# Decoding the second MoE's weights: an even schedule, VectorE in place of GpSimd, and four PSUM banks for h

## The chip, the cores and the metric

The program runs on one core of a Trainium2 chip. The metric is the device time of one execution in microseconds (us). The engines are named as in the profile: PE is TensorE (PEld its weight loads), DVE is VectorE, ACT is ScalarE, POOL is GpSimd, and SP is SyncE, which here only issues DMAs.

## The reference

Three layers follow each other in float32: an attention, and two mixtures that are plain dense layers ("MoE" in the names).

```python
x = attention(q, k, v)                 # 4 batches x 576 tokens = 2304 rows of 512
h = x @ w_in                           # first MoE: 512 -> 2048
x = (h - tanh(h)) @ w_out              # 2048 -> 512
xn = x / sqrt(mean(x*x) + 1e-6) * rms_g
g, val = xn @ w_gate, xn @ w_val       # second MoE: 512 -> 1536, twice
out = (g * sigmoid(g) * val) @ w_out2  # 1536 -> 512
```

The weights arrive as float64. The kernel reads their bits as pairs of 32-bit words and builds float32 values from them on the chip.

## The kernel before

**Weights.** Each weight tile is 128 x 512 values. `Weight.load` (L119) lets SP load its 512 KB. `Weight.bits` (L126) makes a float32 out of the two words: a multiplication by 2 to the power -111 into the tile `ca`, on ACT (L131) or on POOL (L133), then three bit operations on DVE into the tile `ct` (L138, L139, L142). `Weight.split` (L147) writes two float32r parts: the high part is a copy on ACT (L150), the low part a subtraction (L151) on the engine that the stream's `place` names. `ca` and `ct` have two buffers each. A `Stream` (L153) walks through a list of weights: step i loads some weights ahead, decodes weight i and splits weight i - 1. `st1` carries the 32 weights of the first MoE, all on ACT and DVE. `st2` (L195) carries the 36 of the second one (gate, val and out2 for each of 12 blocks f): every other multiplication is on POOL, and two of three subtractions (24 in all) are on POOL. A weight needs a buffer of the pool `wts` for its raw words and one for its parts; `wts` has 32 buffers, and in the second MoE's decode they become free as the last group of the first MoE uses up that MoE's weights. The last five split weights go to a pool of their own (`wts2`).

**First MoE.** The rows are worked on in five groups of 512 (one of 256). For each group and each of 16 blocks f, `unit` (L831) issues: `pe_h` (12 matmuls of 128 x 512 into a PSUM bank of the pool `ps_h`, which has two), tanh on ACT (`tg`, L646), a DVE operation that reads the bank and leaves h - tanh(h) (L651), the high part `g` on ACT (L657), the low part on DVE (L662), and, two units later, `pe_x` (12 matmuls that add to four banks of `ps_x`). In the last group `unit` also moves `st2` on, two weights per block, and `prep(0)` normalises the first 512 rows for the second MoE: squares on ACT, sums on DVE, a matmul with ones, three Newton steps for the inverse root on DVE, and the split of the result into `xn` (L744, L745).

**Second MoE.** It goes through five blocks of rows (four of 512, one of 256). For each f, `pe_gv` issues 12 matmuls for the gate (into `ps_h`) and 12 for the value (into `ps_m`, two banks), silu on ACT (`s`, L762), the product on DVE (L763), and its split (`p`, ACT L765, DVE L766); `pe_o` adds 12 matmuls of the block f before. During the first rows `st2` decodes what is left.

**Order.** The calls above give instructions and their priority; a list scheduler of the framework, which works with modelled times, then sets the order in which they stand on each engine. Each engine runs its row strictly in that order, and so does SP with the DMA issues: an instruction that waits holds all behind it.

Of the kernel before, what the change touches and what calls it, by code (L numbers as in the profile page):

```python
# [7 lines left out]
F32 = mybir.dt.float32  # L8
# [17 lines left out]
def attn_moe_moe_kernel(  # L26
# [22 lines left out]
    nc = tc.nc  # L49
    B, _, NC, D = q_str.shape  # L50
    NT, DM = out.shape
    FA = w_in.shape[0]
    FB = w_gate.shape[0]
# [10 lines left out]
    NG = len(groups)  # L64
# [19 lines left out]
    wts = ctx.enter_context(tc.tile_pool(name="wts", bufs=2 * FA))  # L84
    cvt = ctx.enter_context(tc.tile_pool(name="cvt", bufs=2))
    ps_h = ctx.enter_context(tc.tile_pool(name="ps_h", bufs=2, space=PSUM))
    ps_m = ctx.enter_context(tc.tile_pool(name="ps_m", bufs=2, space=PSUM))
# [22 lines left out]
    def mm(out_, lhsT, rhs, start, stop):  # L110
        nc.tensor.matmul(out_, lhsT, rhs, start=start, stop=stop, skip_group_check=True)  # L111
# [69 lines left out]
    w2 = {(kd, f): Weight(kd, f) for f in range(FB) for kd in ("gate", "val", "out2")}  # L181
    w1_order = [("in", 0)]
    for f in range(1, FA):
# [7 lines left out]
    )  # L191
    w2_order = [w2[kd, f] for f in range(FB) for kd in ("gate", "val", "out2")]
    N2 = 5
    NK = len(w2_order) - N2
    st2 = Stream(  # L195
        w2_order,
        lambda i: ((wts, "w") if i < NK else (wts2, "w2")) + (nc.vector if i % 3 == 0 else nc.gpsimd,),
        3, 2 * FA, lambda i: i % 2 == 0,
    )

    xh = {}
# [432 lines left out]
    xs, g_of, h_of, t_of, xacc = {}, {}, {}, {}, {}  # L634

    def pe_h(g, f, a, e):
        ps = ps_h.tile([128, 512], F32, tag="h", name="ps_h")[:, :e - a]
        w, x = w1["in", f].t, xs[g]
        seq = [(i, k, c) for c in range(4) for i, k in ((0, 0), (0, 1), (1, 0))]
        for n, (i, k, c) in enumerate(seq):  # L640
            mm(ps, w[:, i, c, :], x[:, k, c, a:e], n == 0, n == len(seq) - 1)
        h_of[g, f, a] = ps

    def act_tanh(g, f, a, e):
        t = gp.tile([128, 512], F32, tag="tg", name="tg")[:, :e - a]
        nc.scalar.activation(out=t, in_=h_of[g, f, a], func=ACTF.Tanh, scale=WS)  # L646
        t_of[g, f, a] = t

    def dve_g(g, f, a, e):
        t = t_of[g, f, a]  # L650
        nc.vector.scalar_tensor_tensor(  # L651
            out=t, in0=h_of.pop((g, f, a)), scalar=WS, in1=t, op0=ALU.mult, op1=ALU.subtract
        )

    def g_hi(g, f, a, e):
        t = ghl.tile([128, 2, 512], F32R, tag="g", name="g")[:, :, :e - a]
        nc.scalar.copy(out=t[:, 0], in_=t_of[g, f, a])  # L657
        g_of[g, f, a] = t

    def g_lo(g, f, a, e):  # L660
        t = g_of[g, f, a]
        nc.vector.tensor_tensor(out=t[:, 1], in0=t_of.pop((g, f, a)), in1=t[:, 0].bitcast(F32), op=ALU.subtract)  # L662

    def pe_x(g, f, a, e):
        if g not in xacc:
            xacc[g] = [ps_x.tile([128, 512], F32, tag="x", name="ps_x") for _ in range(4)]
        w, t = w1["out", f].t, g_of.pop((g, f, a))
        for c in range(4):
            for n, (i, k) in enumerate(((0, 0), (1, 0), (0, 1))):
                mm(  # L670
                    xacc[g][c][:, a:e], w[:, i, c, :], t[:, k],
                    f == 0 and n == 0 and a == 0, f == FA - 1 and n == 2,
                )
        if f == FA - 1 and e == width[g]:
            evac_x(g)
# [75 lines left out]
    def pe_gv(j, f):  # L751
        r, n = [], rows[j][1]
        for kd, pool, tag in (("gate", ps_h, "h"), ("val", ps_m, "m")):
            ps = pool.tile([128, 512], F32, tag=tag, name="ps_" + tag)[:, :n]
            w, x = w2[kd, f].t, xn[j]
            seq = [(a, e, c) for c in range(4) for a, e in ((0, 0), (0, 1), (1, 0))]
            for i, (a, e, c) in enumerate(seq):
                mm(ps, w[:, a, c, :], x[:, e, c, :], i == 0, i == len(seq) - 1)
            r.append(ps)
            if kd == "gate":  # L760
                s = pb.tile([128, 512], F32, tag="s", name="s")[:, :n]
                nc.scalar.activation(out=s, in_=ps, func=ACTF.Silu, scale=WS)  # L762
        nc.vector.scalar_tensor_tensor(out=s, in0=r[1], scalar=WS, in1=s, op0=ALU.mult, op1=ALU.mult)  # L763
        t = pb.tile([128, 2, 512], F32R, tag="p", name="p")[:, :, :n]
        nc.scalar.copy(out=t[:, 0], in_=s)  # L765
        nc.vector.tensor_tensor(out=t[:, 1], in0=s, in1=t[:, 0].bitcast(F32), op=ALU.subtract)  # L766
        p_of[j, f] = t

    def pe_o(j, f):
        if f == 0:  # L770
            oacc[j] = [ps_x.tile([128, 512], F32, tag="x", name="ps_x") for _ in range(rows[j][1] // 128)]
        w, p = w2["out2", f].t.rearrange("p s c f -> p s (c f)"), p_of.pop((j, f))
        for t in range(rows[j][1] // 128):
            for i, (a, e) in enumerate(((0, 0), (1, 0), (0, 1))):
                mm(
                    oacc[j][t], p[:, e, t * 128:t * 128 + 128], w[:, a, :],
                    f == 0 and i == 0, f == FB - 1 and i == 2,
                )

    def evac_o(j):  # L780
        if j == nb - 1:
            os = pbx.tile([128, 4, 512], F32, tag="x2", name="os")
        for t in range(rows[j][1] // 128):
            o = os[:, t] if j == nb - 1 else pb.tile([128, 512], F32, tag="o", name="o")
            if t % 2 == 0:
                nc.scalar.mul(out=o, in_=oacc[j][t], mul=WS)
            else:
                nc.vector.tensor_scalar_mul(out=o, in0=oacc[j][t], scalar1=WS)
            t0 = rows[j][0] + t * 128
            nc.sync.dma_start(out=out[t0:t0 + 128, :], in_=o)  # L790
# [32 lines left out]
    def attend(j):  # L823
        w = wks[j]
        if j < EA and len(w.pe) == 12:
            for c in ("abcde" if j == 0 else "ABCDE") + "t":
                ensure(c)
        if w.pe:
            w.pe.pop(0)()

    def unit(g, f, a, e, pe_work=lambda: None, work=lambda: None):  # L831
        if g == 0:
            for i in range(1 if e == SUB else 2):
                while wks[i].pe:
                    attend(i)
            st1.to(w1_at["in", f] + 1)
        pe_h(g, f, a, e)
        act_tanh(g, f, a, e)
        pe_work()
        dve_g(g, f, a, e)  # L840
        work()
        g_hi(g, f, a, e)
        if g == NG - 1 and f >= 1:
            st2.to(min(NK, 2 * f))
        g_lo(g, f, a, e)
        xq.append((g, f, a, e))
        while len(xq) > (1 if g == 0 else 2):
            if xq[0][0] == 0:
                st1.to(w1_at["out", xq[0][1]] + 1)
            pe_x(*xq.pop(0))  # L850

    for c in START:
        if c in "abcdeABCDEt":
            ensure(c)
        elif c == "w":
            st1.load_to(min(st1.n + 1, 2 * FA))
        elif c in "01":
            attend(int(c))
        elif c == "s":
            st1.step()  # L860
        elif c == "U":
            unit(*units.pop(0))
# [5 lines left out]
    for g, f, a, e in units:  # L868
# [16 lines left out]
        def pe_work():  # L885
            if f >= 2 or 0 < g < NG - 1:
                wk.run_pe(max(rem, 1))

        def work():
            if f >= 6 or 0 < g < NG - 1:  # L890
                wk.run(wk.st, max(rem, 1))

        unit(g, f, a, e, pe_work, work)
        if g == NG - 1:
            if f == 4:
# [9 lines left out]
    pbn = ctx.enter_context(tc.tile_pool(name="pbn", bufs=1, reuse_waits="tile"))  # L905
    wts2 = ctx.enter_context(tc.tile_pool(name="wts2", bufs=N2, reuse_waits="tile"))

    pq = []
    for j in range(nb):
        pg = prep(j + 1, pbn if j % 2 == 0 else pbx) if j + 1 < nb else iter(())  # L910
        for f in range(FB):
            if j == 0:
                st2.to(3 * (f + 2))
            pe_gv(j, f)
            if f >= (1 if j > 0 else 4):
                next(pg, None)
                next(pg, None)
            pq.append((j, f))
            if len(pq) > 1:
                jj, ff = pq.pop(0)  # L920
                pe_o(jj, ff)
                if ff == FB - 1:
                    evac_o(jj)
        for _ in pg:
            pass
# [82 lines left out]
```

## Time and profile before

| | |
|---|---|
| three runs | 961.97 us median (961.53 to 963.13) |
| profiled execution | 962.53 us, span from first to last instruction 960.8 us |
| mean granted TensorE clock | 0.994 |
| PE busy | 929.7 us (97%), 5274 matmuls |
| DVE busy | 519.9 us (54%) |
| ACT busy | 346.5 us (36%) |
| POOL busy | 119.6 us (12%), 147 instructions |

PE is the engine that is nearly always busy, so the span is PE's work and the gaps in it. The shares of the other engines are means over stages that differ much: the attention, the decode of weights, and the long second MoE in which only PE has much to do. The last group of the first MoE starts on PE at 400.82 us and the second MoE at about 498 us.

### The profile page before, as it was taken

Reading aid. Unit: us, or ns where it says so; the run is one execution under the profiler, and the core shown is the slowest. Engines: PE = TensorE matmul, PEld = TensorE weight load, DVE = VectorE, ACT = ScalarE, POOL = GpSimd, SP = SyncE. Lnnn points to the kernel's source line nnn. Section 1 sums busy time; section 2 is a strip of 40 time slices with the busy share of each in tenths; the row PEclk is TensorE's granted clock in tenths of the full one; section 3 lists DMA queues with packets and bytes.
Section 4 is the critical chain, followed back from the end, with each engine's and each line's share of the span. In section 5 each row is a group of like instructions: output and inputs, shape, how many; then the busy total and the mean of one; then the engine's idle time right before and its main releaser. Section 6 shows DMA issues by size and latency. Waiting matters only on the chain.

```text
span 960.8 us, 13712 instructions
## 1 busy us (share of the span) xinstructions
PE 929.7 (97%) x5274; PEld 779.3 (81%) x5274; DVE 519.9 (54%) x1199; ACT 346.5 (36%) x820; POOL 119.6 (12%) x147
## 2 busy tenths in 40 slices
PE   5799999999999999999899999999999999999998
PEld 5688888888999888887667778888888888888897
DVE  4899998873454433269999764254124412331212
ACT  4776654223554433244445323113111311121211
POOL 2000036760000000013334210000000000000000
PEclk9799999999999999999999999999999999999999
DMA  9936334220421200066335211101010000000100
GB/s 204 336 127 209 109 104 141 77 79 1 122 84 42 77 31 1 23 219 200 129 105 181 71 39 44 44 1 44 1 44 1 23 1 33 11 1 1 43 2 23
DMA packets 51489, 72.66 MB, mean 76 GB/s; under 512 B 24928, under 2 KB 35552, under 8 KB 51424
## 3 DMA queue, kind: packets, MB, share of 16 engines
q1 hardware_dynamic: 51424, 71.80, 24.5%
q8 instruction: 41, 0.67, 0.3%
q14 instruction: 24, 0.20, 0.1%
HBM read 62.34 MB, written 9.44 MB: 75 GB/s over the span
## 4 chain that ended last, share of the span: by engine, by line
PE 78%; DVE 11%; DMA 5%; issue 3%; POOL 1%; SPq 1%; ACT 1%; POOLq 0%; ACTq 0%
PE ps_h L111 30%; PE ps_x L111 30%; PE ps_m L111 14%; PE ps_s L111 2%; DVE ct L139 2%; DVE ct L142 2%; DVE ct L138 2%; PE ps_v L111 2%; DMA raw<-in_w_out_dram 2%; DVE w L151 1%; DMA raw<-in_w_val_dram 1%; DVE g L662 1%; PE ps_p L325 1%; DMA qz<-in_q_loc_dram 1%; DMA x<-x2d 1%
## 5 line engine op out<-in xcount | busy, mean ns | idle before, releaser
L111 PE MATMUL ps_h<-xs,w 128*128 128x512 f32 (+1 forms) x984 | 220.9, 369 | 6.2 <-DVE tg L651 6.0
L111 PE MATMUL ps_x<-g,w 128*128 128x512 f32 (+1 forms) x984 | 222.0, 368 | 0.6 <-DVE g L662 0.5
L111 PEld LDWEIGHTS ps_h<-xs,w 128*128 128x128 f32 x984 | 169.7, 190 | 37.9 <-DVE tg L651 9.2
L111 PEld LDWEIGHTS ps_x<-g,w 128*128 128x128 f32 x984 | 168.5, 188 | 31.4 <-DVE g L662 1.9
L111 PE MATMUL ps_x<-w,p 128*128 128x512 f32 x648 | 158.9, 392 | 3.5 <-DVE p L766 2.2
L111 PE MATMUL ps_m<-xn,w 128*128 128x512 f32 (+1 forms) x720 | 158.4, 368 | 0.8 <-DVE xn L745 0.8
L111 PE MATMUL ps_h<-xn,w 128*128 128x512 f32 (+1 forms) x720 | 159.0, 369 | 0.1
L763 DVE SCALAR_TENSOR_TENSOR s<-ps_m,s 128x512 f32<-128x512 f32 (+1 forms) x60 | 38.2, 637 | 221.6 <-PE ps_m L111 219.3
L111 PEld LDWEIGHTS ps_h<-xn,w 128*128 128x128 f32 x720 | 126.8, 188 | 24.8 <-DVE tg L651 0.4
L111 PEld LDWEIGHTS ps_m<-xn,w 128*128 128x128 f32 x720 | 126.0, 188 | 24.3 <-DVE xn L745 1.2
L111 PEld LDWEIGHTS ps_x<-w,p 128*128 128x128 f32 x648 | 120.4, 188 | 30.6 <-DVE p L766 3.5
L651 DVE SCALAR_TENSOR_TENSOR tg<-ps_h,tg 128x512 f32<-128x512 f32 (+1 forms) x82 | 50.9, 620 | 86.5 <-ACT tg L646 86.5
L762 ACT ACTIVATE s<-ps_h 128x512 f32<-128x512 f32 (+1 forms) x60 | 33.3, 555 | 158.9 <-PE ps_h L111 158.9
L646 ACT ACTIVATE tg<-ps_h 128x512 f32<-128x512 f32 (+1 forms) x82 | 44.5, 543 | 98.0 <-PE ps_h L111 94.3
L765 ACT CAST p<-s 128x512 fp32r<-128x512 f32 (+1 forms) x60 | 34.6, 577 | 124.1 <-DVE s L763 124.1
L657 ACT CAST g<-tg 128x512 fp32r<-128x512 f32 (+1 forms) x82 | 46.6, 569 | 51.5 <-DVE tg L651 51.4
L662 DVE TENSOR_TENSOR g<-tg,g 128x512 fp32r<-128x512 f32 (+1 forms) x82 | 55.3, 674 | 16.9 <-ACT g L657 16.6
L150 ACT CAST w<-ct 128x512 fp32r<-128x512 f32 x68 | 42.1, 620 | 45.0 <-DVE ct L142 42.5
L766 DVE TENSOR_TENSOR p<-s,p 128x512 fp32r<-128x512 f32 (+1 forms) x60 | 38.7, 645 | 25.8 <-ACT p L765 25.6
L139 DVE SCALAR_TENSOR_TENSOR ct<-ca,ct 128x512 uint32<-128x512 uint32 x68 | 52.1, 767 | 0.7
L142 DVE SCALAR_TENSOR_TENSOR ct<-raw,ct 128x512 uint32<-128x512 uint32 x68 | 51.7, 761 | 0.4
L131 ACT ACTIVATE ca<-raw 128x512 f32<-128x512 f32 x50 | 33.7, 674 | 35.1 <-DVE ct L139 18.0
(89 smaller groups left out, 723.1 us busy)
## 6 DMA issues: line engine op xcount, KB each, us to landing
raw<-in_w_out_dram SPq DMA_DIRECT2D x28, 512.0 KB, 5.8
raw<-in_w_in_dram SPq DMA_DIRECT2D x16, 512.0 KB, 8.7
raw<-in_w_gate_dram SPq DMA_DIRECT2D x12, 512.0 KB, 4.0
raw<-in_w_val_dram SPq DMA_DIRECT2D x12, 512.0 KB, 3.8
x2d<-xe SPq DMA_DIRECT2D x36, 128.0 KB, 1.9
x<-x2d SPq DMA_DIRECT2D x16, 256.0 KB, 4.2
out_dram<-o SPq DMA_DIRECT2D x16, 256.0 KB, 2.0
v<-in_v_loc_dram SPq DMA_DIRECT2D x14, 192.0 KB, 2.6
```

The source lines that it names most:

```text
L111: nc.tensor.matmul(out_, lhsT, rhs, start=start, stop=stop, skip_group_check=True)
L131: nc.scalar.mul(out=a, in_=hi.bitcast(F32), mul=2.0 ** -111)
L139: nc.vector.scalar_tensor_tensor(out=t, in0=a, scalar=0x80000000, in1=t, op0=ALU.bitwise_and, op1=ALU.bitwise_or)
L142: nc.vector.scalar_tensor_tensor(out=t, in0=lo, scalar=29, in1=t, op0=ALU.logical_shift_right, op1=ALU.bitwise_or)
L150: nc.scalar.copy(out=t[:, 0], in_=self.b)
L646: nc.scalar.activation(out=t, in_=h_of[g, f, a], func=ACTF.Tanh, scale=WS)
L651: nc.vector.scalar_tensor_tensor(out=t, in0=h_of.pop((g, f, a)), scalar=WS, in1=t, op0=ALU.mult, op1=ALU.subtract)
L657: nc.scalar.copy(out=t[:, 0], in_=t_of[g, f, a])
L662: nc.vector.tensor_tensor(out=t[:, 1], in0=t_of.pop((g, f, a)), in1=t[:, 0].bitcast(F32), op=ALU.subtract)
L763: nc.vector.scalar_tensor_tensor(out=s, in0=r[1], scalar=WS, in1=s, op0=ALU.mult, op1=ALU.mult)
L765: nc.scalar.copy(out=t[:, 0], in_=s)
L766: nc.vector.tensor_tensor(out=t[:, 1], in0=s, in1=t[:, 0].bitcast(F32), op=ALU.subtract)
```

## The change

Four edits. All subtractions of `st2` go to DVE, and all its multiplications to ACT. The number of weights that `unit` asks for in the last group falls from two per block to 18 in 15 blocks. In the first 512 rows of the second MoE the remaining 18 are asked for evenly. And in the last group the blocks with odd f take their bank for h from `ps_m`, so that four banks take turns.

```diff
--- before.py
+++ after.py
@@ -191,11 +191,12 @@
     )
     w2_order = [w2[kd, f] for f in range(FB) for kd in ("gate", "val", "out2")]
     N2 = 5
+    N1 = 18
     NK = len(w2_order) - N2
     st2 = Stream(
         w2_order,
-        lambda i: ((wts, "w") if i < NK else (wts2, "w2")) + (nc.vector if i % 3 == 0 else nc.gpsimd,),
-        3, 2 * FA, lambda i: i % 2 == 0,
+        lambda i: ((wts, "w") if i < NK else (wts2, "w2")) + (nc.vector,),
+        3, 2 * FA, lambda i: True,
     )
 
     xh = {}
@@ -634,7 +635,8 @@
     xs, g_of, h_of, t_of, xacc = {}, {}, {}, {}, {}
 
     def pe_h(g, f, a, e):
-        ps = ps_h.tile([128, 512], F32, tag="h", name="ps_h")[:, :e - a]
+        pool, tag = (ps_m, "m") if g == NG - 1 and f % 2 else (ps_h, "h")
+        ps = pool.tile([128, 512], F32, tag=tag, name="ps_h")[:, :e - a]
         w, x = w1["in", f].t, xs[g]
         seq = [(i, k, c) for c in range(4) for i, k in ((0, 0), (0, 1), (1, 0))]
         for n, (i, k, c) in enumerate(seq):
@@ -841,7 +843,7 @@
         work()
         g_hi(g, f, a, e)
         if g == NG - 1 and f >= 1:
-            st2.to(min(NK, 2 * f))
+            st2.to(N1 * f // (FA - 1))
         g_lo(g, f, a, e)
         xq.append((g, f, a, e))
         while len(xq) > (1 if g == 0 else 2):
@@ -910,7 +912,7 @@
         pg = prep(j + 1, pbn if j % 2 == 0 else pbx) if j + 1 < nb else iter(())
         for f in range(FB):
             if j == 0:
-                st2.to(3 * (f + 2))
+                st2.to(max(3 * (f + 2), N1 + (len(w2_order) - N1) * (f + 1) // (FB - 1)))
             pe_gv(j, f)
             if f >= (1 if j > 0 else 4):
                 next(pg, None)
```

Because a scheduler sets the order, three places show what it made of this. The first is DVE in the middle of the last group, one unit of the first MoE: from one `tg` (the operation that frees the bank of h) to the next. `ct` rows are the decode of weights, `w` their low parts, `g` the low part of the unit before. Before:

```order
L651 SCALAR_TENSOR_TENSOR tg<-ps_h,tg 128x512
L151 TENSOR_TENSOR w<-ct,w 128x512
L142 SCALAR_TENSOR_TENSOR ct<-raw,ct 128x512
L138 TENSOR_SCALAR ct<-ca 128x512
L662 TENSOR_TENSOR g<-tg,g 128x512
L139 SCALAR_TENSOR_TENSOR ct<-ca,ct 128x512
L142 SCALAR_TENSOR_TENSOR ct<-raw,ct 128x512
L138 TENSOR_SCALAR ct<-ca 128x512
L139 SCALAR_TENSOR_TENSOR ct<-ca,ct 128x512
L651 SCALAR_TENSOR_TENSOR tg<-ps_h,tg 128x512
```

and in the changed kernel:

```order
L653 SCALAR_TENSOR_TENSOR tg<-ps_h,tg 128x512
L142 SCALAR_TENSOR_TENSOR ct<-raw,ct 128x512
L151 TENSOR_TENSOR w<-ct,w 128x512
L664 TENSOR_TENSOR g<-tg,g 128x512
L138 TENSOR_SCALAR ct<-ca 128x512
L151 TENSOR_TENSOR w<-ct,w 128x512
L139 SCALAR_TENSOR_TENSOR ct<-ca,ct 128x512
L138 TENSOR_SCALAR ct<-ca 128x512
L142 SCALAR_TENSOR_TENSOR ct<-raw,ct 128x512
L139 SCALAR_TENSOR_TENSOR ct<-ca,ct 128x512
L653 SCALAR_TENSOR_TENSOR tg<-ps_h,tg 128x512
```

Both decode two weights in a unit here; the changed row has one more `w`, since both low parts are now on DVE (the old unit has one of its low parts on DVE, the others on POOL). Up to the last `tg` of the group, 21 weights had their third bit operation before, and 19 have it now.

The second place is PE at the turn from the first to the second MoE, from the last `ps_h` of the last group on; `xn` are the normalised rows. Before:

```order
L111 MATMUL ps_h<-xs,w 128x512 x12
L111 MATMUL ps_x<-g,w 128x512 x12
L111 MATMUL ps_m<-xn,w 128x512 x2
L111 MATMUL ps_h<-xn,w 128x512 x3
L111 MATMUL ps_x<-g,w 128x512 x8
L111 MATMUL ps_h<-xn,w 128x512 x7
L111 MATMUL ps_x<-g,w 128x512 x4
L111 MATMUL ps_h<-xn,w 128x512 x2
L111 MATMUL ps_x<-g,w 128x512 x12
L111 MATMUL ps_m<-xn,w 128x512 x10
L111 MATMUL ps_h<-xn,w 128x512 x12
L111 MATMUL ps_m<-xn,w 128x512 x12
```

and now:

```order
L111 MATMUL ps_h<-xs,w 128x512 x12
L111 MATMUL ps_x<-g,w 128x512 x20
L111 MATMUL ps_h<-xn,w 128x512
L111 MATMUL ps_m<-xn,w 128x512
L111 MATMUL ps_h<-xn,w 128x512
L111 MATMUL ps_x<-g,w 128x512 x4
L111 MATMUL ps_h<-xn,w 128x512 x3
L111 MATMUL ps_m<-xn,w 128x512 x3
L111 MATMUL ps_h<-xn,w 128x512 x8
L111 MATMUL ps_m<-xn,w 128x512 x5
L111 MATMUL ps_x<-g,w 128x512 x12
L111 MATMUL ps_h<-xn,w 128x512 x2
```

Eight more `ps_x` matmuls of the first MoE now stand ahead of the first matmul that needs `xn`, and gate and value of the first block are interleaved.

The third place is SP's queue around the write of the last group's result (`x2d<-xe`); the `raw` rows are loads of weights, `x<-x2d` is the read of the second 512 rows. Before:

```order
L124 DMA raw<-in_w_out_dram 128x512
L124 DMA raw<-in_w_gate_dram 128x512
L124 DMA raw<-in_w_val_dram 128x512
L703 DMA x_5579<-x2d 128x512 x4
L124 DMA raw<-in_w_out_dram 128x512
L124 DMA raw<-in_w_gate_dram 128x512
L124 DMA raw<-in_w_val_dram 128x512
L689 DMA x2d<-xe 128x256 x6
L124 DMA raw<-in_w_out_dram 128x512
L689 DMA x2d<-xe 128x256 x2
L124 DMA raw<-in_w_gate_dram 128x512
```

and now:

```order
L124 DMA raw<-in_w_out_dram 128x512
L705 DMA x_5539<-x2d 128x512 x2
L124 DMA raw<-in_w_gate_dram 128x512
L705 DMA x_5539<-x2d 128x512 x2
L124 DMA raw<-in_w_val_dram 128x512
L124 DMA raw<-in_w_out_dram 128x512
L691 DMA x2d<-xe 128x256 x8
L124 DMA raw<-in_w_gate_dram 128x512
L124 DMA raw<-in_w_val_dram 128x512
```

The write now goes out in one piece of eight, behind 27 of the 36 weight loads and not 29, so nine loads follow it and not seven.

## Rows read from the trace of the kernel before

**Rows 1.** The tensor engine's waits, 395 to 620 us: total, times, longest (us)

```profile
PE ps_h L111 <- DVE tg L651: 5.9, 6, 1.7
PE ps_x L111 <- DVE p L766: 2.2, 3, 1.2
PE ps_x L111 <- ACT p L765: 1.3, 1, 1.3
PE ps_m L111 <- DVE xn L745: 0.8, 1, 0.8
PE ps_x L111 <- DVE g L662: 0.5, 2, 0.3
```

**Rows 2.** Busy time of the engines in three stretches

```profile
core 0: us, PE busy (x) PEld busy (x) DVE busy (x) ACT busy (x) POOL busy (x), PEclk, DMA share, GB/s
62.00:100.00 38.00, 38.00 (x277) 31.54 (x275) 36.64 (x85) 25.54 (x60) 1.04 (x2) 1.00 0.59 183
437.10:517.60 80.50, 73.03 (x305) 56.02 (x303) 78.94 (x115) 38.98 (x65) 32.06 (x24) 1.00 0.46 151
518.00:565.00 47.00, 43.77 (x187) 34.84 (x188) 32.52 (x49) 15.96 (x27) 16.12 (x13) 1.00 0.27 85
```

**Rows 3.** Timeline of PE, 436 to 572 us: start, us, instructions [idle]

```profile
438.90 2.88 PE L111 MATMUL ps_h<-xs,w 128*128 128x512 f32 x12
441.62 2.88 PE L111 MATMUL ps_x<-g,w 128*128 128x512 f32 x12
445.70 3.02 PE L111 MATMUL ps_h<-xs,w 128*128 128x512 f32 x12 [1.19 <-DVE tg L651]
...
491.45 3.04 PE L111 MATMUL ps_h<-xs,w 128*128 128x512 f32 x12
...
519.01 3.01 PE L111 MATMUL ps_x<-w,p 128*128 128x512 f32 x12 [1.30 <-ACT p L765]
...
536.55 2.58 PE L111 MATMUL ps_x<-w,p 128*128 128x512 f32 x10 [1.20 <-DVE p L766]
...
565.40 2.93 PE L111 MATMUL ps_h<-xn,w 128*128 128x512 f32 x12
568.17 2.91 PE L111 MATMUL ps_m<-xn,w 128*128 128x512 f32 x12
```

**Rows 4.** Timeline of DVE and POOL, 436 to 452 us

```profile
436.11 0.41 DVE L138 TENSOR_SCALAR ct<-ca 128x512 uint32<-128x512 uint32 x1
...
436.45 0.68 DVE L142 SCALAR_TENSOR_TENSOR ct<-raw,ct 128x512 uint32<-128x512 uint32 x1
437.05 0.68 DVE L651 SCALAR_TENSOR_TENSOR tg<-ps_h,tg 128x512 f32<-128x512 f32 x1
...
437.90 1.58 POOL L151 TENSOR_TENSOR w<-ct,w 128x512 fp32r<-128x512 f32 x1 [4.41 <-ACT w L150]
438.36 1.67 DVE L142 SCALAR_TENSOR_TENSOR ct<-raw,ct 128x512 uint32<-128x512 uint32 x1
...
444.96 0.68 DVE L651 SCALAR_TENSOR_TENSOR tg<-ps_h,tg 128x512 f32<-128x512 f32 x1
...
451.33 0.68 DVE L651 SCALAR_TENSOR_TENSOR tg<-ps_h,tg 128x512 f32<-128x512 f32 x1
```

**Rows 5.** DVE by line, 62 to 100 us (count, busy us, mean ns, idle before)

```profile
L139 DVE SCALAR_TENSOR_TENSOR ct<-ca,ct 128x512 uint32<-128x512 uint32 x12 | 8.2, 683 | 0.0
...
L651 DVE SCALAR_TENSOR_TENSOR tg<-ps_h,tg 128x512 f32<-128x512 f32 x5 | 3.4, 688 | 0.9 <-ACT tg L646 0.9
```

**Rows 6.** DVE by line, 437 to 518 us

```profile
L139 DVE SCALAR_TENSOR_TENSOR ct<-ca,ct 128x512 uint32<-128x512 uint32 x20 | 18.0, 901 | 0.2
```

**Rows 7.** Timeline of SP's DMA issues, 536 to 560 us

```profile
543.97 0.33 SPq L124 DMA_DIRECT2D raw<-in_w_gate_dram  x1
550.72 0.33 SPq L124 DMA_DIRECT2D raw<-in_w_val_dram  x1
556.86 0.33 SPq L124 DMA_DIRECT2D raw<-in_w_out_dram  x1
```

## The prediction

> **What bounds the kernel now.** I read the waits of PE first. Between 395 and 620 us they come to 10.7 us in all, 5.9 of it on `ps_h` for DVE's `tg` and the rest on `p`, `xn` and `g`, which DVE and ACT deliver [rows 1]. The windows come next: from 437.10 to 517.60 us DVE is busy 78.94 of 80.50 us, PE 73.03, ACT 38.98, and POOL 32.06 [rows 2]. So in this stretch, the second half of the last group and the turn to the second MoE, DVE sets the pace and PE waits for it. The granted clock is 1.00 (2.4 GHz) in all three windows, so no clock is to be won back.
>
> The reader should then see in PE's timeline what the waits cost. An undisturbed block of 12 matmuls takes 2.72 us (438.90 to 441.62) in the first MoE and 2.77 us (565.40 to 568.17) in the first rows of the second [rows 3]. The block due at 444.34 starts at 445.70: 1.36 us late, where the view names 1.19 us of idle time, since the restart is slow too. I therefore count by starts. From 441.62 to 491.45 us, 49.83 us, PE's row holds 182 matmuls (eight blocks of `ps_x`, seven of `ps_h`, two with ones): 182 x 2.72 / 12 = 41.25 us, so 8.6 us are lost. From 491.45 to 565.40 us, 73.95 us, it holds 290: 48 of the first MoE are 10.9 us, 242 of the second at 2.77 / 12 are 55.9 us, and 7.2 us are lost. The sum, 15.8 us, is all that this change can give back; before 441.62 and behind 565.40 it touches no stretch in which PE waits for DVE's decode.
>
> Why is DVE so slow there? Its start-to-start times are 0.34 us for the short operation L138 (436.11 to 436.45) and 0.60 us for one of the long kind (436.45 to 437.05) [rows 4]. From the `tg` at 437.05 to the first product of the second MoE (which starts at 517.63 us, just behind the window's end) its row has 22 short and 92 long ones: 22 x 0.34 + 92 x 0.60 = 62.7 us. They took 80.6 us, a factor of 1.286. The long ones are stretched while POOL works: L142 at 438.36 lasts 1.67 us and not 0.68, and a subtraction on POOL runs from 437.90 for 1.58 us [rows 4]. L139 lasts 901 ns on average here [rows 6], but 683 ns from 62 to 100 us [rows 5].
>
> That earlier stretch is the best witness. There the first MoE's weights are decoded just as the changed kernel decodes the second's: all multiplications on ACT, all subtractions on DVE. DVE is busy 36.64 of 38.00 us, POOL 1.04, and PE 38.00 of 38.00 [rows 2]. A full DVE without POOL's company holds PE up by nothing.
>
> **The change part by part.** *POOL's subtractions to DVE.* This adds 24 operations of 0.60 us, 14.4 us in all. Between the same two marks (the sixth `tg` and the first product) the changed row has 20 short and 98 long operations: 6.8 + 58.8 = 65.6 us, 2.9 more than before, since three weights fewer are decoded there. PE's own work between these marks is ten units of 5.44 us, 0.45 us for the ones, and 63 matmuls from the last `ps_h` of the group on (14.3 us): 69.2 us. DVE's 65.6 us fit, with 95% of the time used, about the share of the witness (96%). Without the stretching, DVE no longer sets the pace.
>
> *POOL's multiplications to ACT.* 18 operations of the ACT kind at about 0.68 us are 12 us over some 165 us. ACT is busy 48% in the worst window [rows 2], which hides them. What it does not hide is the order: a `tanh` behind a multiplication that waits for `ca` makes DVE wait for ACT. In the witness this cost DVE 0.9 us before five `tg` operations [rows 5] and PE nothing.
>
> *The even schedule.* The order shows little of it: 19 weights instead of 21 are decoded by the last `tg`, and two weights a unit stay the rule in the middle of the group. The scheduler takes decode work as soon as buffers are free. In the first 512 rows DVE has 42.3 us of work from the first to the eighth product where PE has seven blocks of 8.3 us, 58 us. I give it no price of its own.
>
> *Four banks.* With two banks, the `ps_h` two units on needs `tg` within three blocks, 8.2 us, of the end of its own. With four that wait goes, but `ps_x` of the same unit stands directly behind that `ps_h` and needs `g`, which is later than `tg` by one ACT and at least one DVE operation. So the banks give one block of room at most, once: between 0 and 2.7 us. I take 0, the bound nearer to a DVE that keeps pace.
>
> *What stays lost.* In the last group, between nothing and the witness's idle share (0.9 of 38.00 us, here 1.4 us): I take 0.5, as there PE lost none of it. At the turn eight more `ps_x` matmuls (1.8 us) stand ahead of the first need of `xn`, against a wait of 0.8 us now; between 0 and 3 us, I take 0.7. For `p`, now 3.5 us of waits and about 1.2 us of slow restarts: between 0 and 4.7 us. DVE's rows between a product and its `p` still hold decode operations, which wait for loads, so I take 0.9. SP issues the read of the second rows earlier relative to two weight loads; these rows are wanted tens of us later, so I give it nothing. Together 2.1 us.
>
> The sum: 15.8 - 2.1 = 13.7 us. The profiled execution took 962.53 us, 0.56 above the median of 961.97; against the median this makes 948.3 us.
>
> **The rivals.** *The chain of the last loads (faster, but less).* Near the end of the decode only one buffer is free for raw words. The loads at 543.97, 550.72 and 556.86 us follow each other at 6.75 and 6.14 us [rows 7], each behind the decode of the weight ahead of it. In the changed order nine loads, not seven, follow the write of the last group. If all nine go one by one, they take 55 to 61 us, and DVE's row wants the last of them before its eighth product, 58 us behind the first. Since ACT and DVE wait in order, silu and `p` would stand behind multiplications whose load is late. For it: the `p` wait of 1.20 us at 536.55 [rows 3]. Against it: the first loads have more than one buffer, and each `p` has some 3 us of slack behind its product. Price: 5 us on top, 953.3 us.
>
> *DVE stays as slow as it is (slower).* If the stretching is not POOL's doing but comes with decode, DMA traffic and ACT on the same memory, the factor of 1.286 stays, and the heavier row takes 65.6 x 1.286 = 84.4 us instead of 80.6: 3.8 us slower, 965.8 us. It decides from a factor of 80.6 / 65.6 = 1.23 on. Against it stands the witness, with the same mix, DMA at 183 GB/s (here 151) and no stretching. The Trainium skill says on this (SBUF — State Buffer, section "SBUF: two separate sides") that only VectorE and GpSimd share a pair of ports, as a lock that one instruction holds to its end, and that ScalarE and DMA never contend for it; the 1.67 us operation agrees. By that rule all of POOL's 32.06 us could be blocked time, where the rows give 17.9 us; PE's loss caps either, so the sum stays, and this rival alone would fall to nothing.
>
> *No change.* The decode isn't spread, as the order shows. If the wins in the last group come back as waits at the turn, `xn` and `p` each late by their present waits and the loads' chain on top, the time stays near 962 us. For it: DVE has only 3.6 us to spare between the marks. Against it: the witness has less.
>
> **How the numbers follow.** The forecast has 0.63, the chain of loads 0.22, no change 0.08, slower 0.07. A difference under 0.2% (1.9 us) can't be told from no change here. Faster: 0.63 + 0.22 = 0.85; same 0.08; slower 0.07. The forecast's own range is 946.2 (all 15.8 us back) to 951.5. The range that should hold 8 in 10 takes in the chain of loads: 946.0 to 957.0.
>
> **What would show it.** L139 and its like near 683 ns from 437 us on. The last `ps_h` of the last group starting at about 483 us, not 491.45. PE busy nearly throughout that stretch, no wait on `tg`, and the second MoE reached some 10 us earlier. If L139 stays near 900 ns with POOL idle, the slower rival holds. If the last group is clean but waits on `p` grow between 510 and 570 us behind L138 that waits for ACT's `ca`, the chain of loads holds. The forecast is wrong if PE still loses over 7 us between 441 us and the eighth block of the second MoE.

## The result, and the profile after

The changed kernel takes 947.04 us (median of four runs, 946.10 to 947.45), the kernel before on the same chip 961.75 us (961.31 to 963.13). The ratio is 0.9843, with a 95% interval from 0.9826 to 0.9860. Forecast were 948.3 us, and 946.0 to 957.0 as the range.

The profiled execution took 946.10 us, its span is 944.3 us. On its page, the busy time of the engines and the shares of the chain of waits:

```profile
PE 927.7 (98%) x5274; PEld 782.9 (83%) x5274; DVE 510.5 (54%) x1223; ACT 357.9 (38%) x838; POOL 65.2 (7%) x105
...
PE 94%; DVE 2%; DMA 1%; SPq 1%; issue 0%; ACT 0%
```

PE's share of the chain was 78% before and is 94% now, DVE's fell from 11% to 2%, and POOL has 42 operations fewer. PE's own waits between 395 and 620 us, five rows before [rows 1], are none at all: the view is empty in that stretch, and what PE still waits for lies in the first 50 us.

The windows, the first the witness of the prediction, the second from where the sixth `tg` stood before (437.05 us; here it starts at 434.38) to just before the first `ps_x<-w,p` block of the second MoE (columns as in [rows 2]):

```profile
core 0: us, PE busy (x) PEld busy (x) DVE busy (x) ACT busy (x) POOL busy (x), PEclk, DMA share, GB/s
62.00:100.00 38.00, 38.00 (x279) 31.63 (x278) 36.62 (x89) 25.55 (x59) 1.04 (x2) 1.00 0.58 184
437.10:508.00 70.90, 70.90 (x313) 58.52 (x312) 68.97 (x124) 44.39 (x75) 0.00 (x0) 1.00 0.49 164
```

PE is busy 70.90 of 70.90 us, where it was 73.03 of 80.50. DVE is as full as before, 68.97 of 70.90, but it holds nothing up. ACT rose from a share of 48% to one of 63%.

The timeline of PE shows when the stages begin (start, us, instructions):

```profile
400.34 2.88 PE L111 MATMUL ps_h<-xs,w 128*128 128x512 f32 x12
...
438.42 2.88 PE L111 MATMUL ps_h<-xs,w 128*128 128x512 f32 x12
441.14 2.88 PE L111 MATMUL ps_x<-g,w 128*128 128x512 f32 x12
...
482.44 2.88 PE L111 MATMUL ps_h<-xs,w 128*128 128x512 f32 x12
...
508.52 2.89 PE L111 MATMUL ps_x<-w,p 128*128 128x512 f32 x12
...
548.96 2.93 PE L111 MATMUL ps_h<-xn,w 128*128 128x512 f32 x12
551.73 1.54 PE L111 MATMUL ps_m<-xn,w 128*128 128x512 f32 x6
```

These answer to [rows 3]. The last `ps_h` of the last group starts at 482.44 us (before 491.45), the first `ps_x<-w,p` at 508.52 (before 519.01), and the block that stood at 565.40 starts at 548.96. So 16.44 us are won by then; 0.48 of them were there when the last group began (400.34, before 400.82), and 15.96 come from the stretch that the change touches. Its start-to-start times are 2.72 us throughout the first MoE and 2.72 or 2.77 in the second.

DVE by line from 437 to 508 us (count, busy us, mean ns, idle before):

```profile
L151 DVE TENSOR_TENSOR w<-ct,w 128x512 fp32r<-128x512 f32 x19 | 13.1, 692 | 0.0
L139 DVE SCALAR_TENSOR_TENSOR ct<-ca,ct 128x512 uint32<-128x512 uint32 x18 | 12.5, 692 | 0.0
...
L653 DVE SCALAR_TENSOR_TENSOR tg<-ps_h,tg 128x512 f32<-128x512 f32 x10 | 6.9, 694 | 0.0
```

L139 fell from 901 ns [rows 6] to 692, near the 683 of the witness [rows 5], with its like beside it.

The chain of the last loads, the second likeliest case, is in the trace. DVE's longest waits from 420 to 570 us (us, times, longest):

```profile
DVE ct L138 <- ACT ca L131: 8.1, 4, 3.5
```

and SP's issues behind the write of the last group's result:

```profile
500.02 4.27 SPq L691 DMA_DIRECT2D x2d<-xe  x8
504.33 0.45 SPq L124 DMA_DIRECT2D raw<-in_w_gate_dram  x1
...
511.40 0.33 SPq L124 DMA_DIRECT2D raw<-in_w_gate_dram  x1
...
533.84 0.33 SPq L124 DMA_DIRECT2D raw<-in_w_gate_dram  x1
541.04 0.33 SPq L124 DMA_DIRECT2D raw<-in_w_val_dram  x1
547.32 0.33 SPq L124 DMA_DIRECT2D raw<-in_w_out_dram  x1
```

The last loads are 7.20 and 6.28 us apart, about as far as in [rows 7], and L138 waits 8.1 us for the multiplications that stand behind them. But from the first issue to the last the nine loads need 43 us, where nine gaps of that size would be 55 to 61: the first three go out within 2.7 us, right behind the write, the fourth 4.4 us later and the rest one by one. No `p` is late enough for PE to notice.

### The profile page after: what moved, and what is told of

Read it like the earlier page. It is cut to its first block, busy times and chain, and to the rows that moved or that the text cites. A ratio compares the mean times of both kernels' runs of the same rounds, so it can differ in the third digit from the quotient of the medians.

```text
span 944.3 us, 13675 instructions
## 1 busy us (share of the span) xinstructions
PE 927.7 (98%) x5274; PEld 782.9 (83%) x5274; DVE 510.5 (54%) x1223; ACT 357.9 (38%) x838; POOL 65.2 (7%) x105
## 4 chain that ended last, share of the span: by engine, by line
PE 94%; DVE 2%; DMA 1%; SPq 1%; issue 0%; ACT 0%
PE ps_x L111 37%; PE ps_h L111 37%; PE ps_m L111 16%; PE ps_s L111 2%; PE ps_v L111 2%; DMA raw<-in_w_in_dram 1%; PE ps_p L326 1%; PE ps_p L426 1%; DVE ct L142 0%; DVE ct L139 0%; SPq L241 0%; DVE w L151 0%; SPq L379 0%; DVE ct L138 0%; DVE sm L297 0%
## 5 line engine op out<-in xcount | busy, mean ns | idle before, releaser
L664 DVE TENSOR_TENSOR g<-tg,g 128x512 fp32r<-128x512 f32 (+1 forms) x82 | 53.4, 651 | 17.0 <-ACT g L659 16.6
L131 ACT ACTIVATE ca<-raw 128x512 f32<-128x512 f32 x68 | 45.7, 674 | 42.4 <-DVE ct L139 18.6
L151 DVE TENSOR_TENSOR w<-ct,w 128x512 fp32r<-128x512 f32 x68 | 46.5, 689 | 3.0 <-ACT w L150 2.8
L139 DVE SCALAR_TENSOR_TENSOR ct<-ca,ct 128x512 uint32<-128x512 uint32 x68 | 46.6, 689 | 0.2
```

The costliest lines, as they stand in the source:

```text
L131: nc.scalar.mul(out=a, in_=hi.bitcast(F32), mul=2.0 ** -111)
L139: nc.vector.scalar_tensor_tensor(out=t, in0=a, scalar=0x80000000, in1=t, op0=ALU.bitwise_and, op1=ALU.bitwise_or)
L151: lo_eng.tensor_tensor(out=t[:, 1], in0=self.b, in1=t[:, 0].bitcast(F32), op=ALU.subtract)
```

## One measure for all runs

Executions of one kernel differ by some 2 us in their first stretch: the first `ps_h` of the last group starts at 400.34 us in the profile above and at 402.72 in another of the same kernel. From that start to the end of the span the kernels can be compared without this scatter:

| kernel | first `ps_h` of the last group | span | from there to the end |
|---|---|---|---|
| before | 400.82 | 960.8 | 560.0 |
| changed | 400.34 | 944.3 | 544.0 |
| changed, again | 402.72 | 946.7 | 544.0 |
| GpSimd's work away alone (e1_off) | 400.29 | 944.3 | 544.0 |
| four banks alone (e3_banks) | 401.36 | 960.9 | 559.5 |
| changed, multiplications back on GpSimd (e7_mul) | 401.12 | 945.1 | 544.0 |
| changed, subtractions back on GpSimd (e10_sub) | 399.96 | 952.9 | 552.9 |
| changed + 18 two-input operations on GpSimd (e4_company) | 399.44 | 955.5 | 556.1 |
| changed + 18 one-input operations on GpSimd (e8_company1) | 400.66 | 947.8 | 547.1 |
| changed + 18 two-input operations on DVE (e11_dve) | 398.87 | 942.9 | 544.0 |

Four kernels, in five executions of this table, share the 544.0 us: PE's own work without a gap. The change is worth 16.0 us by this measure; the medians, with the scatter, say 14.7.

## The experiments

**GpSimd's work away, and nothing else (e1_off).** The kernel before with every multiplication on ACT and every subtraction on DVE; two banks and the old pace of asking stay.

```diff
-        lambda i: ((wts, "w") if i < NK else (wts2, "w2")) + (nc.vector if i % 3 == 0 else nc.gpsimd,),
-        3, 2 * FA, lambda i: i % 2 == 0,
+        lambda i: ((wts, "w") if i < NK else (wts2, "w2")) + (nc.vector,),
+        3, 2 * FA, lambda i: True,
```

> The kernel before with one edit alone: the second MoE's multiplications all on ACT and its subtractions all on DVE (GpSimd off); asking pace and two banks for h as before. The order of DVE, POOL and SP is then that of the changed kernel, row for row. Theory (GpSimd's company is the whole cause): 947 to 949 us, all of the change's gain but 0 to 1 us for the banks; no wait of PE on tg. Rival (the four banks carry part of the gain): 951 to 957 us, with waits of PE on tg in the last group.

Measured: 946.51 us (946.05 to 947.62), 0.9841 of before [0.9825, 0.9858]. PE has no wait from 395 to 620 us, and the window reads (PE, PEld, DVE, ACT, POOL, clock, DMA share, GB/s):

```profile
437.00:508.00 71.00, 71.00 (x313) 58.58 (x312) 69.22 (x124) 44.63 (x75) 0.00 (x0) 1.00 0.51 164
```

This is the whole gain: the four banks and the even schedule add nothing to it. The even schedule could not add anything, since it moves nothing: added alone to the kernel before, or taken out of the changed one, it leaves every engine's row as it was, waits included. For that reason it was not run.

**Four banks alone (e3_banks).**

```diff
-        ps = ps_h.tile([128, 512], F32, tag="h", name="ps_h")[:, :e - a]
+        pool, tag = (ps_m, "m") if g == NG - 1 and f % 2 else (ps_h, "h")
+        ps = pool.tile([128, 512], F32, tag=tag, name="ps_h")[:, :e - a]
```

> The kernel before with the four banks alone. DVE's order is that of before, row for row. Theory: DVE still sets the pace through the last group, so the waits on tg turn into waits of ps_x on g one block later, and at most 2.7 us come back, once: 959 to 962 us. Rival (banks carry the gain): 950 to 956 us.

Measured: 962.52 us (960.86 to 963.07), ratio 1.0001 [0.9992, 1.0010]. PE's waits from 395 to 620 us (us, times, longest):

```profile
PE ps_x L111 <- DVE g L663: 4.4, 4, 1.7
PE ps_x L111 <- DVE p L767: 2.6, 3, 1.2
PE ps_h L111 <- DVE tg L652: 2.0, 1, 2.0
PE ps_x L111 <- ACT p L766: 1.5, 1, 1.5
```

Compare [rows 1]. The waits on `tg` fell from 5.9 to 2.0 us, those on `g` rose from 0.5 to 4.4. More room in front of a DVE that is too slow only moves the place where PE waits for it.

**GpSimd's company, added (e4_company).** The changed kernel with 18 subtractions on GpSimd in the last group that nobody needs (each reads the high part of a weight twice and writes a scratch tile). No other instruction moves in any row.

```diff
+            if "scr" in company:
+                h = t[:, 0].bitcast(F32)
+                nc.gpsimd.tensor_tensor(out=company["scr"], in0=h, in1=h, op=ALU.subtract)
```

> The changed kernel with 18 additional GpSimd subtractions in the last group (two inputs read from the weight's high part, the output to a scratch tile that nothing reads); no other engine's row differs and nothing waits for them. Theory (GpSimd's company stretches DVE): DVE's long operations rise from 692 ns to 800 to 900 ns between 437 us and the first product; 18 times about 1 us is more than the 3.6 us that DVE has to spare plus some 3 us of lag, so 8 to 12 us are lost: 955 to 959 us. Rival (the stretching comes from decode, DMA traffic and ACT on the same memory): 947 us as the changed kernel, DVE's operations at 690 ns.

Measured: 957.67 us (956.28 to 958.53), 0.9952 of before [0.9937, 0.9967], so 10.6 us slower than the changed kernel by the medians, and 12.1 us (556.1 against 544.0) from the last group on. DVE by line from 437 to 514 us:

```profile
L142 DVE SCALAR_TENSOR_TENSOR ct<-raw,ct 128x512 uint32<-128x512 uint32 x17 | 13.7, 806 | 0.0
...
L138 DVE TENSOR_SCALAR ct<-ca 128x512 uint32<-128x512 uint32 x18 | 11.5, 637 | 0.0
...
L657 DVE SCALAR_TENSOR_TENSOR tg<-ps_h,tg 128x512 f32<-128x512 f32 x10 | 6.8, 677 | 0.0
```

From the sixth `tg` (436.2 us) to the first product (513.82) DVE's 65.6 us of work take 77.6; in the changed kernel, from 434.38 to 502.46, they take 68.1. The 800 to 900 ns expected for DVE's long operations did not come to all of them: L142 has 806, L139 keeps 679 in this run, so it matters which operation stands where GpSimd starts. And PE waits again:

```profile
PE ps_x L111 <- DVE g L668: 4.5, 5, 1.5
PE ps_h L111 <- ACT s L768: 2.0, 1, 2.0
PE ps_h L111 <- DVE tg L657: 1.4, 1, 1.4
```

DVE's instructions, the DMA traffic and ACT's work are those of the changed kernel. So it is GpSimd's operations that stretch DVE's, and the slower rival (the stretching comes with decode and traffic) falls. How they do it stands in single rows, GpSimd and DVE together:

```profile
436.47 1.04 POOL L154 TENSOR_TENSOR scr<-w 128x512 f32<-128x512 f32 x1 [1.95 <-ACT w L150]
436.80 1.00 DVE L138 TENSOR_SCALAR ct<-ca 128x512 uint32<-128x512 uint32 x1
...
441.07 0.68 DVE L657 SCALAR_TENSOR_TENSOR tg<-ps_h,tg 128x512 f32<-128x512 f32 x1
...
441.34 1.04 POOL L154 TENSOR_TENSOR scr<-w 128x512 f32<-128x512 f32 x1 [3.82 <-ACT w L150]
441.67 1.26 DVE L142 SCALAR_TENSOR_TENSOR ct<-raw,ct 128x512 uint32<-128x512 uint32 x1
```

The operation on POOL at 436.47 ends at 437.51; L138, started at 436.80, ends 0.29 us later and not after 0.41. The next ends at 442.38, and L142 ends 0.55 us behind that. DVE's operation gets nowhere until GpSimd's is over. All 18 operations of GpSimd hold one of DVE's in this way. The 14 held between the marks take 9.2 us more, added up, than the same operations in the changed kernel, which is nearly all of the 9.5 us (77.6 less 68.1). [rows 4] show the same: POOL's subtraction of 437.90 ends at 439.48, L142 ends at 440.03, again 0.55 us later. `tg` escapes: at 441.07 it keeps its 0.68 us beside POOL, and its mean over the stretch is 677 ns. It reads one input from PSUM and one from SBUF; the operations that are held read SBUF alone.

**The same with one input (e8_company1).** The 18 operations scale a tile instead of subtracting two.

```diff
-                nc.gpsimd.tensor_tensor(out=company["scr"], in0=h, in1=h, op=ALU.subtract)
+                nc.gpsimd.tensor_scalar(
+                    out=company["scr"], in0=h, scalar1=0.5, scalar2=1.0, op0=ALU.mult, op1=ALU.mult
+                )
```

> As the run before, but the 18 additional GpSimd operations read one input (a scaling) and not two. Theory: they last about 0.65 us as the old multiplications did and hold DVE by 0.1 to 0.5 us each, 2 to 9 us in all, most of which DVE's spare time covers: 947 to 951 us, DVE's long operations at 700 to 770 ns. Rival (any GpSimd operation costs DVE its whole length): 18 x 0.65 = 12 us, 952 to 955 us. Second rival (only operations with two inputs contend): 947 us, 690 ns.

Measured: 949.51 us (948.10 to 950.48), 0.9867 [0.9853, 0.9882], 2.5 us slower than the changed kernel by the medians (3.1 from the last group on). PE's waits from 395 to 620 us, and one meeting of POOL and DVE:

```profile
PE ps_h L111 <- ACT s L770: 1.7, 1, 1.7
PE ps_x L111 <- DVE g L670: 0.6, 1, 0.6
```

```profile
441.31 0.63 POOL L154 TENSOR_SCALAR scr<-w 128x512 f32<-128x512 f32 x1 [3.82 <-ACT w L150]
...
441.63 0.85 DVE L142 SCALAR_TENSOR_TENSOR ct<-raw,ct 128x512 uint32<-128x512 uint32 x1
```

DVE is held here too: POOL ends at 441.94 and L142 at 442.48, 0.54 us later. But the operation is over in 0.63 us and not in 1.04: begun 0.32 us ahead of L142, about as in the company above (0.33), it leaves 0.31 us to wait and not 0.71. The rest of the expectation missed: the 18 operations last 1.68 us on average, not 0.65. The last five fill 20.3 us from 467.69 us on; there GpSimd is the one that waits. The 1.7 us on `s` are silu behind ACT's squares, which waited 2.47 us for their rows from memory. The changed kernel has the same wait, 2.44 us, and PE does not notice it there. What differs is when: counted from the first `ps_h` of the last group, the read of these rows goes out at 95.00 us and not at 90.04, and silu starts at 106.44 and not at 101.49. The read is released by DVE, which the company has made 5 us late. So this wait, like the 0.6 us on `g` and the 2.0 us on `s` in the company above (read at 102.05 us), comes from GpSimd's company by way of a late DVE.

**The multiplications back on GpSimd (e7_mul).**

```diff
-        3, 2 * FA, lambda i: True,
+        3, 2 * FA, lambda i: i % 2 == 0,
```

> The changed kernel with every other multiplication of the second MoE's decode back on GpSimd (18 operations with one input); the rows of DVE, PE and SP are those of the changed kernel. Theory: one-input operations on GpSimd cost DVE little, as the 18 added ones with one input did (2.5 us of time): 947.5 to 950 us. Rival (GpSimd's multiplications carry a good part of the gain, since decode waits for them in DVE's row): 952 to 957 us, with DVE waiting at L138 for GpSimd.

Measured: 945.86 us (945.28 to 946.87), 0.9827 [0.9806, 0.9847]; no wait of PE from 395 to 620 us. It missed on the good side: GpSimd is busy 26.1 us with 18 multiplications in all, and none of it costs PE anything. POOL and DVE's `tg` operations, in the first meeting with the two operations ahead of `tg`:

```profile
444.08 1.92 POOL L133 TENSOR_SCALAR ca<-raw 128x512 f32<-128x512 f32 x1 [3.57 <-issue]
444.19 0.68 DVE L142 SCALAR_TENSOR_TENSOR ct<-raw,ct 128x512 uint32<-128x512 uint32 x1
444.79 0.68 DVE L139 SCALAR_TENSOR_TENSOR ct<-ca,ct 128x512 uint32<-128x512 uint32 x1
...
445.39 0.68 DVE L653 SCALAR_TENSOR_TENSOR tg<-ps_h,tg 128x512 f32<-128x512 f32 x1
...
449.56 1.92 POOL L133 TENSOR_SCALAR ca<-raw 128x512 f32<-128x512 f32 x1 [3.57 <-DVE ct L139]
...
450.88 0.68 DVE L653 SCALAR_TENSOR_TENSOR tg<-ps_h,tg 128x512 f32<-128x512 f32 x1
...
455.04 1.32 POOL L133 TENSOR_SCALAR ca<-raw 128x512 f32<-128x512 f32 x1 [3.57 <-DVE ct L139]
...
455.76 0.68 DVE L653 SCALAR_TENSOR_TENSOR tg<-ps_h,tg 128x512 f32<-128x512 f32 x1
```

A multiplication needs 0.65 us, yet these take 1.92 and 1.32. The three end at 446.00, 451.48 and 456.36 us, the `tg` operations at 446.07, 451.56 and 456.44: as if each multiplication waited until DVE came to the one operation that leaves GpSimd alone, and ran beside that. L142 and L139, which read SBUF alone, pass first at their usual 0.68 us, with no turn for GpSimd between them. On average DVE's L139 keeps 679 ns. Here lies the difference to the subtraction: 0.65 us are over with `tg`, whose turn on DVE is 0.60 us long, while the 1.04 us of the subtraction run on into the next operation and hold it. Six of the 18 multiplications still hold one, where in the company all 18 did.

**The subtractions back on GpSimd (e10_sub).** 24 of the 36, as before; all multiplications stay on ACT.

```diff
-        lambda i: ((wts, "w") if i < NK else (wts2, "w2")) + (nc.vector,),
+        lambda i: ((wts, "w") if i < NK else (wts2, "w2")) + (nc.vector if i % 3 == 0 else nc.gpsimd,),
```

> The changed kernel with two of three subtractions of the second MoE's decode back on GpSimd (24 operations with two inputs), all multiplications on ACT. Theory: these 24 are what stretches DVE; the time lies 2 to 4 us under the kernel before: 957.5 to 960 us, with waits of PE on tg or g in the last group. Rival (subtractions and multiplications share the loss evenly): 952 to 956 us.

Measured: 957.65 us (954.72 to 957.93), 0.9944 [0.9922, 0.9966]. PE's waits, and one line of DVE from 437 to 514 us:

```profile
PE ps_x L111 <- DVE g L664: 2.6, 3, 1.2
PE ps_h L111 <- DVE tg L653: 1.4, 1, 1.4
PE ps_x L111 <- DVE p L768: 1.1, 1, 1.1
PE ps_h L111 <- DVE xn L747: 0.8, 1, 0.8
PE ps_x L111 <- ACT p L767: 0.4, 1, 0.4
```

```profile
L139 DVE SCALAR_TENSOR_TENSOR ct<-ca,ct 128x512 uint32<-128x512 uint32 x21 | 21.7, 1035 | 0.2
```

The waits of [rows 1] are back, 6.3 us of the 10.7, and L139, which here stands where the subtractions start, is stretched to 1035 ns. By the medians the subtractions alone cost 10.6 us and the multiplications on top of them 4.8 (962.43 before, less 957.65); by the profiled execution, the quickest of its four, it is 8.9 and 7.1. (The second figure holds what four banks give as well, nothing or 0.5 us by e3_banks.) The time lies at the edge of the theory's 957.5 to 960 us, but 4.8 us under the kernel before and not 2 to 4, and the profiled execution (954.72) lies in the rival's range. So the subtractions carry the larger part, and not the whole, as the theory had it; how much larger, 8.9 or 10.6 us, these four executions leave open. The multiplications that are free by themselves are not free beside subtractions. Two rows of before, between those of [rows 4], show why:

```profile
439.45 1.09 POOL L133 TENSOR_SCALAR ca<-raw 128x512 f32<-128x512 f32 x1
439.95 1.14 DVE L662 TENSOR_TENSOR g<-tg,g 128x512 fp32r<-128x512 f32 x1
```

The multiplication starts as the subtraction of 437.90 ends (439.48), while DVE's L142 is still at work until 440.03, and so the next operation of DVE is held in its turn: the multiplication ends at 440.54 us, L662 at 441.09, again 0.55 us later.

**The same operations on DVE (e11_dve).** The 18 extra subtractions of the company on DVE itself.

```diff
-                nc.gpsimd.tensor_tensor(out=company["scr"], in0=h, in1=h, op=ALU.subtract)
+                nc.vector.tensor_tensor(out=company["scr"], in0=h, in1=h, op=ALU.subtract)
```

> The changed kernel with the 18 additional subtractions with two inputs of the earlier run given to DVE, and not to GpSimd; the scheduler makes room by decoding fewer weights in the last group (16 by its last tg, not 19). Theory: 18 x 0.60 us are 10.8 us of DVE work; between the marks DVE's row grows to 66.6 us only, under PE's 69.2, so 946 to 949 us: the same operation that costs about 10 us on GpSimd is hidden on DVE. Rival (DVE has no more than 3.6 us to spare, wherever the decode goes): 952 to 955 us, with waits on tg, g or p.

Measured: 945.88 us (944.64 to 946.26), 0.9827 [0.9808, 0.9845]; no wait of PE from 395 to 620 us. DVE from 437 to 514 us:

```profile
L139 DVE SCALAR_TENSOR_TENSOR ct<-ca,ct 128x512 uint32<-128x512 uint32 x17 | 11.7, 690 | 0.0
...
L154 DVE TENSOR_TENSOR scr<-w 128x512 f32<-128x512 f32 x14 | 9.7, 691 | 0.0
```

Fourteen more operations of 691 ns in a DVE that was 97% busy cost nothing. The rows say why: the scheduler decodes 16 weights by the last `tg` and not 19, the others later, where there is room. The same operation costs 10.6 us on the engine that has nothing to do. (It does not show that DVE has 10 us to spare; the work was moved.)

**The changed kernel and the best variant again, side by side (e12_changed and e13_mul_again).** The changed kernel, and the one with the multiplications on GpSimd, with no further edit.

> The changed kernel once more, beside the next run on one chip. Theory: no wait of PE behind 395 us; what differs between it and the next run is the first 50 us alone, 945.5 to 947.5 us.

> The changed kernel with 18 multiplications on GpSimd, once more, on the same chip as the run before. Theory: the place of the multiplications is worth nothing while the subtractions are on DVE: within 1 us of the run before, with no wait of PE behind 395 us. Rival (GpSimd's help with them is a gain): 1 to 2 us faster than the run before, with intervals that do not overlap.

Measured: 947.92 us (946.25 to 948.48), 0.9845 [0.9829, 0.9861], and 947.07 us (946.05 to 947.74), 0.9838 [0.9823, 0.9853]. They are the same, as expected; with 544.0 us for both from the last group on, nothing is left there for either to win. (The medians of e1_off, e3_banks, e11_dve and e12_changed lie 0.1 to 0.5 us outside the ranges expected, which is less than the scatter of the first stretch.)

## Why the prediction was right, point by point

- *What bounds the kernel.* Right. The 15.8 us counted from the starts of PE's blocks are the 15.96 us that came back. The 10.7 us of named waits would have been too few.
- *The stretching is POOL's doing.* Right, and now shown by adding it back with everything else in place (e4_company). The witness stretch had said so: same decode, same traffic, no POOL, no stretching. The 17.9 us were not all POOL's, though: the held operations of before take 14.8 us more than the same ones in the changed kernel, DVE is idle for 1.6 us of the stretch, and the rest is not accounted for.
- *Subtractions to DVE.* Right: 65.6 us of work in 68.1 us, where PE needs about 69. Of the 2.5 us above the sum, 1.9 are two waits for ACT's squares.
- *Multiplications to ACT.* Right that ACT hides them; the waits of L138 for ACT are 8.1 us from 420 to 570 us and cost PE nothing. Alone they could as well have stayed (e7_mul).
- *The even schedule, no price.* Right; it moves no instruction.
- *Four banks, 0 to 2.7 us, taken as 0.* Right: 0 with a DVE that keeps pace (e1_off), and 0.5 us or less without (559.5 against 560.0, within the medians' scatter).
- *What stays lost, 2.1 us.* This term was mis-sized: it measured 0. In the last group 0.5 was taken and 0.05 measured; at the turn 0.7, and `p` 0.9, and PE has no wait for either. Each was a share of a wait of before, kept as if it belonged to the place. They all had one cause, the late DVE, and went with it.
- *The read of the second rows, no price.* The price held, the reason did not: these rows are wanted at once and not tens of us later. ACT's squares stand ready for them (a wait of 2.44 us) and silu stands behind the squares. With a DVE that keeps pace PE does not notice; with a late one it loses 1.7 us (e8_company1) or 2.0 (e4_company).
- *The chain of last loads (22%).* Its mechanism is there and its price isn't. It let nine loads go one by one from the first on; three had buffers at once, and the others fitted beside PE.
- *Slower (7%) and no change (8%).* Both out. The point from which the slower one decides was a factor of 1.23; it measured 68.1 / 65.6 = 1.04.

The forecast of 948.3 us against 947.04 is thus closer than its working: the profiled pair shows 16.4 us (962.53 to 946.10) where the sum said 13.7, and the median of the changed kernel happens to lie 0.9 us above its profiled execution.

## What to carry to other kernels

Where a full VectorE and a GpSimd work out of SBUF at once, look at VectorE's mean times with and without GpSimd's company before counting GpSimd's share as help: here 24 subtractions of 0.60 us each, moved off VectorE, made the kernel 8.9 to 10.6 us slower. Count a loss by starts of blocks over the whole stretch, and when its cause goes, expect the small waits at its edges to go too. And look at the order of the instructions before pricing an edit: one of the four here moved nothing.

## What the runs showed of the hardware that was not expected

The prediction took it that GpSimd's 32.06 us of busy time held DVE for 17.9 us, a part. Operation by operation it is all or nothing: in before, e4_company, e8_company1, e7_mul and e10_sub every held operation of DVE ends 0.53 to 0.56 us (two inputs) or 0.28 to 0.29 us (one input) after GpSimd's does. The total is smaller because some of GpSimd's busy time is its own waiting (as with the multiplication of 0.65 us that is on record for 1.92 in e7_mul) and some lies beside `tg`. The Trainium skill (SBUF — State Buffer, section "SBUF: two separate sides") states this lock for a VectorE operation in a two-port mode or with two SBUF inputs, held "for the whole instruction" by whichever starts first; these rows agree, and `tg`, with one input in PSUM, goes free in every kernel here (677 to 694 ns on average).

Not settled: L138 has one input and is held all the same (637 ns on average in e4_company, not 428). It is also the quick one, 0.34 us from start to start against 0.60; whether it runs in such a two-port mode, no run here tells. And in all kernels the first and third block of rows of the second MoE have 2.76 or 2.77 us per 12 matmuls of 128 x 512 where the second and fourth have 2.72, at a granted clock of 1.00 (the fifth block has 256 rows and no like to compare); no run here tries that.
